# Attention and experts on one core: another order for the first three pairs of heads

## The chip, the cores and the metric

The kernel runs on one core of a Trainium2 chip. The metric is the device time in microseconds (us) of one execution, as the median of several runs. Beside those runs one execution was profiled: its trace tells for every engine when each instruction ran. The engines are TensorE (PE; its weight loads are shown apart as PEld), VectorE (DVE), ScalarE (ACT), GpSimd (POOL) and SyncE (SP), which issues most of the transfers.

## The reference

The program is an attention over 64 heads, and behind it a routed expert layer. The change touches the attention alone. Its arithmetic is this (8 batches of 8 heads, 1152 keys of 64 elements, queries pooled in twos to 576):

```python
def _attn_ref(q, k, v) -> np.ndarray:
    B, H, S, D = q.shape
    factor = 2
    scale = 1.0 / np.sqrt(D)
    q_pool = q.reshape(B, H, S // factor, factor, D).mean(axis=3)
    scores = scale * np.matmul(q_pool, k.transpose(0, 1, 3, 2))
    scores = scores - np.max(scores, axis=-1, keepdims=True)
    attn = np.exp(scores)
    attn = attn / (np.sum(attn, axis=-1, keepdims=True) + 1e-09)
    return np.matmul(attn, v).astype(np.float32)
```

The result goes, as x of 4608 rows, to the expert layer: a gate product, a greedy assignment of each row to one of 8 experts with room for 576 rows each, and two products with a relu between them for each expert.

## The kernel before

The 64 heads are worked on as 32 pairs, numbered 0 to 31. A pair has 18 score steps, nine blocks of 128 keys for each of its two heads; step g of the program is step g mod 18 of pair g // 18. A step (function `step`) has four parts. PE makes the scores of 128 keys against 576 queries, four products into one of the two score banks `sc` (L751). ACT takes their exponential into a buffer P (L754). POOL, or for a few steps DVE, writes what the rounding of P leaves over into a buffer PM (L758). PE then multiplies P and PM with the values into a bank `av` (L768, 15 products; "AV" below). There are ten P and ten PM buffers. POOL takes the PM parts of all 18 steps of pair 0.

Softmax here doesn't subtract the exact maximum while scores come. Before a pair's scores start, an upper bound for each query is found. PE multiplies the pair's rounded queries and keys (L668, L678, for pair 0 L659) into the banks `ma` and `mb`, DVE takes the maximum of each (L671, L680, L662), folds the maxima (L703, for pair 0 L699) and, after a transposition on PE (L723, L713), writes them as extra rows that the scores take in (L724 and a transfer; for pair 0 L717 and L720). So the bounds of pair n+1 are made while the steps of pair n run. Keys and queries are split into a rounded half (KH, QH) and a rest (KL, QL), and spread to where the scores want them by transfers that SP issues (L617). Values are split in the same way (V; L634 to L645). From pair 2 on the rests are made by DVE (KL: L610, QL: L591, V: L645); for pairs 0 and 1 by POOL (L578 to L606, L638). Once a pair POOL also issues a transfer that adds the second query of each two to the first (L486).

What stands at the start besides: memsets on POOL (L459 to L463, among them the row of KB buffers that the extra rows are multiplied with, L461), and on PE 23 products of constants (L891, "fillers"), which are made for no result. Every second pair the finished attention output is transposed on PE (L803), copied by ACT (L806) and multiplied with the gate weights (L815).

The order on every engine is made ahead of the run by `Cycle.plan`: each item has a tag and a number within its tag and pair, a table gives a time for it, and items are taken by that time as soon as what they need has been taken. Table `TAU` is for all pairs, with 25 times the pair's number added; `TAU0`, `TAU1` and `TAU2` hold the entries of pairs 0, 1 and 2. Engines and queues work in the order so written: an instruction that waits holds up all that stand behind it on its engine, and a transfer that waits holds up SP's later ones.

Of the kernel before, what the change touches and what calls it, by code (L numbers as in the profile page):

```python
# [152 lines left out]
class Cycle(Order):  # L153
# [11 lines left out]
    def plan(self):  # L165
# [44 lines left out]
       [2.7664, 4.9823, 6.5534, 8.0795, 9.6086, -181.5656, 16.9348, 19.0221, 21.216], "qkb": [5.2308, 7.0644, 8.3738,  # L210
       12.1143, 0.0557, 20.0132, 22.5039, 25.3261, 28.3165], "ql": [-38.1313], "rc": [9.2364, -9.47], "sc":
       [-36.4174], "scv": [-30.065], "spr": [-21.9235, -31.1405, -21.9627, -26.5265, -22.5479, -164.2155, -315.3032,
       -74.6622, -15.1485, -17.1123, -19.956, -16.4269], "store": [-95.7261], "sx": [16.3692, 22.2312, 0.8466,
       -61.2066, -78.1894], "tab": [-60.4], "tad": [-127.8336], "tap": [-44.6145, -41.1498, -47.4908, -31.2065],
       "vh": [-26.7285, -47.8828], "vl": [-23.1603, -21.3115], "vs": [-148.6017, -208.4574], "vsh": [-168.3274],
       "wsq": [12.8365], "x": [-94.3595, -7.6786]}
TAU0 = {"abk": [-60.377, -62.9993], "abs": [-96.8953, -53.0217], "aug": [-7.39949, -0.804], "augt": [-7.399491,
# [133 lines left out]
def attention(ctx, tc, top, kt, qt, v, wg, w1, x_dram, L, npair=NPAIR):  # L351
# [3 lines left out]
    od = Cycle()  # L355
# [1295 lines left out]
```

## Time and profile before

| what | value |
|---|---|
| median of 3 runs | 1245.68 us (1243.24 to 1245.83) |
| the profiled execution | 1244.15 us, its span in the trace 1242.4 us |
| busy share of the span | PE 96%, DVE 82%, ACT 78%, POOL 73% |
| first exponential of pair 0 | 26.62 us |
| 19th, 37th, 55th, 73rd exponential | 63.50, 90.70, 114.25, 136.58 us |
| attention, 576 exponentials | to about 780 us; the expert layer after that |

The 19th, 37th, 55th and 73rd exponentials mark where pairs 1, 2, 3 and 4 begin. Later on a pair takes 22.3 or 23.4 us in turn; the first three take 36.9, 27.2 and 23.6 us.

### The profile page before, as it was taken

What the parts mean: (1) busy time and instruction counts of PE and PEld (TensorE: products, weight loads), DVE (VectorE), ACT (ScalarE), POOL (GpSimd) and SP (SyncE); (2) the same over time, 40 slices, a digit from 0 to 9 for tenths busy, and PEclk for the clock granted to TensorE, in tenths of its full rate; (3) what the DMA queues carried; (4) which work ended last, traced back from release to release, by engine and by line L of the source; (5) the groups of instructions that cost most, each with busy time, mean ns of one, the idle gap of its engine ahead of it and who ended that gap; (6) DMA issues with size and microseconds to landing.
All of it is one profiled execution on the core that took longest, in us unless ns stands there. A gap on an engine that the chain in (4) does not pass through costs nothing.

```text
span 1242.4 us, 38895 instructions
## 1 busy us (share of the span) xinstructions
PE 1193.8 (96%) x15470; PEld 862.5 (69%) x15470; DVE 1020.9 (82%) x2743; ACT 973.7 (78%) x1719; POOL 901.8 (73%) x879
## 2 busy tenths in 40 slices
PE   7899999998999999999999999789999999999998
PEld 2567777777777787777777778565657466575663
DVE  5889999999999899999999995689888898893520
ACT  6879999998999899999999987055876686776751
POOL 5879898897888898888897898044775584665641
PEclk7999999999999999999999999899999999999999
DMA  6677676776676777776876741042453554547401
GB/s 185 161 177 193 168 186 178 181 188 162 164 183 184 169 179 183 177 179 176 187 185 164 182 98 39 20 174 82 131 192 108 165 183 137 170 135 228 122 31 39
DMA packets 131218, 190.83 MB, mean 154 GB/s; under 512 B 50268, under 2 KB 86108, under 8 KB 128732
## 3 DMA queue, kind: packets, MB, share of 16 engines
q1 hardware_dynamic: 117948, 126.75, 38.8%
q0 software_dynamic: 12944, 61.58, 17.7%
q8 instruction: 121, 1.98, 0.7%
q14 instruction: 61, 0.50, 0.1%
q10 hardware_dynamic: 144, 0.02, 0.0%
HBM read 116.41 MB, written 18.87 MB: 109 GB/s over the span
## 4 chain that ended last, share of the span: by engine, by line
PE 77%; DVE 11%; DMA 5%; ACT 3%; issue 2%; POOL 1%; SPq 0%; POOLq 0%; ACTq 0%; DVEq 0%
PE sc L751 21%; PE av L768 18%; PE ph L1536 11%; PE po L1566 10%; PE mb L668 5%; PE ma L668 5%; DMA W<-in_w_dram,widx 2%; DVE MX L671 2%; PE av L803 1%; ACT P L754 1%; PE av L815 1%; PE rt L1169 1%; DVE HX L1545 1%; DVE GE L1163 1%; PE po L1572 1%
## 5 line engine op out<-in xcount | busy, mean ns | idle before, releaser
L758 POOL TENSOR_TENSOR PM<-P 128x576 f16<-128x576 f32 x508 | 614.3, 1270 | 103.9 <-ACT P L754 53.3
L754 ACT ACTIVATE P<-sc,EX 128x576 f32<-128x576 f32 x576 | 412.8, 739 | 80.4 <-PE sc L751 65.3
L768 PEld LDWEIGHTS <-P 128*128 128x128 bf16 x5760 | 294.5, 98 | 30.6 <-issue 2.3
L768 PE MATMUL av<-V,P 128*128 128x65 f16 (+1 forms) x5760 | 302.7, 192 | 0.0
L768 PE MATMUL av<-V,PM 128*128 128x65 f16 x2880 | 294.1, 194 | 0.0
L768 PEld LDWEIGHTS <-PM 128*128 128x128 f16 x2880 | 264.2, 97 | 0.0
L751 PE MATMUL sc<-QB,KB 65*128 65x288 f16 (+1 forms) x1152 | 236.6, 286 | 0.8 <-DMA QB<-AU 0.8
L751 PE MATMUL sc<-QA,KA 128*128 128x288 f16 x1152 | 235.3, 285 | 1.6 <-ACT P L754 1.3
L671 DVE TENSOR_REDUCE MX<-mb 128x1 f32<-128x512 f32 x279 | 191.0, 685 | 29.2 <-PE mb L668 23.9
L671 DVE TENSOR_REDUCE MX<-ma 128x1 f32<-128x512 f32 x279 | 191.0, 685 | 11.0 <-PE ma L668 7.5
L751 PEld LDWEIGHTS <-KA 128*128 128x128 f16 x1152 | 106.4, 97 | 75.9 <-issue 23.6
L1566 PE MATMUL po<-W2H,HX 128*128 128x512 f16 x512 | 155.5, 379 | 0.0
L1536 PE MATMUL ph<-XH,W1H 128*128 128x320 f16 (+1 forms) x512 | 146.2, 286 | 1.1 <-ACT XH L1425 0.6
L1536 PE MATMUL ph<-XL,W1H 128*128 128x320 f16 (+1 forms) x512 | 146.2, 286 | 0.6 <-DVE XL L1430 0.6
L1536 PE MATMUL ph<-XH,W1L 128*128 128x320 f16 (+1 forms) x512 | 145.9, 286 | 0.0
L751 PEld LDWEIGHTS <-KB 65*128 65x128 f16 (+1 forms) x1152 | 112.8, 98 | 30.9 <-issue 1.0
L1566 PEld LDWEIGHTS <-HX 128*128 128x128 f16 x768 | 71.2, 98 | 78.5 <-issue 0.5
L1536 PEld LDWEIGHTS <-W1H 128*128 128x128 f16 x1024 | 97.9, 98 | 31.0 <-issue 6.4
L1588 POOL DMA_INDIRECT out_dram<-OT,idx x40 | 39.0, 975 | 109.8 <-ACT OT L1568 91.8
L668 PE MATMUL mb<-KH,BD 128*128 128x512 f16 x279 | 106.1, 380 | 6.3 <-DVE AU L724 4.0
L668 PE MATMUL ma<-KH,BD 128*128 128x512 f16 x279 | 106.3, 381 | 4.4 <-DVE MX L671 1.8
L1489 POOL TENSOR_TENSOR W2L<-W,W2H 128x512 f16<-128x512 f32 x64 | 73.1, 1157 | 38.6 <-ACT W L1487 34.1
(308 smaller groups left out, 2159.7 us busy)
## 6 DMA issues: line engine op xcount, KB each, us to landing
KD<-in_kt_dram SPq DMA_DIRECT2D x64, 288.0 KB
VD<-in_v_dram SPq DMA_DIRECT2D x32, 576.0 KB
WB<-in_w_dram SPq DMA_DIRECT2D x32, 512.0 KB
QA<-QH SPq DMA_DIRECT2D x128, 72.0 KB
KA<-KH SPq DMA_DIRECT2D x64, 144.0 KB
KA<-KL SPq DMA_DIRECT2D x64, 144.0 KB
KB<-KH SPq DMA_DIRECT2D x64, 144.0 KB
x_dram<-X SPq DMA_DIRECT2D x16, 576.0 KB
```

What stands on the lines that cost most here:

```text
L668: od.add(t, "PE", 214, lambda: nc.tensor.matmul(m, BD[i][:, j, :], KH[i][:, 512 * c:512 * c + 512], start=True, stop=True), r=bd + [("KH", ...
L671: od.add(t, "DVE", 597, lambda: nc.vector.tensor_reduce(MX[i][:, j, c:c + 1], m, axis=AX.X, op=OP.max), r=[mk], w=[("MX", i, j, c)], tag=" ...
L751: nc.tensor.matmul(c[:, t, :288], a[i][:rows, s, ks], b[i][:rows, s, 288 * t:288 * t + 288], start=first, stop=not first)
L754: od.add(g + 0.1, "ACT", 624, lambda: nc.scalar.activation(p.rearrange("p (t q) -> p t q", t=2), c[:, :, :288], AF.Exp, scale=EX[n % 3][:, ...
L758: od.add(g + 0.2, en, dur, lock=1, fn=lambda: eng.tensor_tensor(pm, p, hi, op=OP.subtract), r=[("P32", g % NP)], w=[("PM", g % NM)], tag="pm")
L768: nc.tensor.matmul(out, w[:, qs], v, start=kb == 0 and j == 0 and y == 0, stop=kb == NKB - 1 and y == 2, skip_group_check=True)
L803: nc.tensor.transpose(m[:, 128 * z:128 * z + 128], X[u][:, 3 * q + z], ident)
L815: nc.tensor.matmul(av[1][32 * q:32 * q + E, :384], wgs[:, c], XT[q].rearrange("p c t -> p (c t)"), start=True, stop=True)
L1489: od.add(tt, "POOL", 1230, lambda o=lo[p], a=raw[p], h=hi[p]: nc.gpsimd.tensor_tensor(o, a, h, op=OP.subtract), r=[key, hk, sk], w=[(nm + ...
L1536: nc.tensor.matmul(p, a[:, d, fs], b[:, d, qs], start=z == 0, stop=z == 11)
L1566: nc.tensor.matmul(o, a[:, z, q0:q0 + 128], b[:, z], start=z == 0 and y == 0, stop=z == 7 and y == 2)
L1588: st = nc.gpsimd.indirect_dma_start(out=out, out_offset=bass.IndirectOffsetOnAxis(ap=idx[i][:n, c:c + 1], axis=0), in_=OT[ob][:n], in_offs ...
```

## The change

The tables `TAU0`, `TAU1` and `TAU2` are written anew, and now hold entries for the score steps of pairs 1 and 2 as well, which took those of `TAU` before. In `TAU` three entries are other numbers: `kh` (the first half of the rounded keys), `kl`, and `gt` (the second of the three gate transpositions). For pair 0 the bound products of the first head go through five banks in a fixed turn (ma, av0, sc0, av1, sc1) where eight were used by a running number. Two starting values of pair 1's items change with it.

Of the tables two lines stand here for all:

```diff
-       [-94.8433], "gt": [23.9764, 39.0716, 42.6939], "kh": [-31.3132, -34.1197], "kl": [-42.4384, -155.424], "ld":
+       [45.877], "gml": [37.3972, 54.4199, 340.2916], "gp": [-94.8433], "gt": [23.9764, 39.35, 42.6939], "kh":
+       [-32.4, -34.1197], "kl": [-32.38, -155.424], "ld": [-70.8466, -187.4708], "ldq": [-65.2457], "ldv":
...
@@ -651,10 +676,10 @@
         i = n % 2
         if n == 0:
             h, j = j // 5, j % 5
-            banks = [(ma, "ma"), (mb, "mb")]
-            if not h:
-                banks += [(sc[a // 2][:, a % 2], ("sc", a // 2, a % 2)) for a in range(4)] + [(av[b], f"av{b}") for b in range(2)]
-            m, mk = banks[z % len(banks)]
+            if h:
+                m, mk = ((ma, "ma"), (mb, "mb"))[z % 2]
+            else:
+                m, mk = ((ma, "ma"), (av[0], "av0"), (sc[0][:, 0], ("sc", 0, 0)), (av[1], "av1"), (sc[1][:, 0], ("sc", 1, 0)))[(5 * c + j) % 5]
...
             if n == 1:
-                at.update(load=-61.5, vload=-57, split=-42.5, bound=-42, spread=-34, val=-36, mm=-20, fold1=1, aug=1.5)
+                at.update(load=-61.5, vload=-57, split=-31.6, bound=-31.15, spread=-23.5, val=-29, mm=-20, fold1=1, aug=1.5)
...
     for g in range(npair * NSTEP):
         od.cur = od.base = g // NSTEP
-        od.zero = int(g < NSTEP)
+        od.zero = (1, 2, 3, 0)[min(g // NSTEP, 3)]
         step(g)
```

The change neither adds nor removes an instruction; line numbers behind the tables are 25 higher after it. From pair 3 on two things stand in another place: every second pair one ACT pass (KH) and one set of gate transpositions on PE. Three places follow.

The first is POOL where pair 0 ends (PM_157 from P_147 is the PM part of step 17, V_104 the rest of pair 1's values, KB_96 the buffer of pair 1 that L461 fills). Before:

```order
L758 TENSOR_TENSOR PM_155<-P_145 128x576
L758 TENSOR_TENSOR PM_157<-P_147 128x576
L758 TENSOR_TENSOR PM_156<-P_146 128x576
L638 TENSOR_TENSOR V_104<-VD_123,V_104 128x9x64 x2
L758 TENSOR_TENSOR PM_158<-P_148 128x576
```

Now:

```order
L783 TENSOR_TENSOR PM_151<-P_141 128x576
L663 TENSOR_TENSOR V_104<-VD_123,V_104 128x9x64 x2
L783 TENSOR_TENSOR PM_153<-P_143 128x576
L783 TENSOR_TENSOR PM_154<-P_144 128x576
L511 DMA QS_125<-in_qt_dram 128x576
L783 TENSOR_TENSOR PM_155<-P_145 128x576
L783 TENSOR_TENSOR PM_156<-P_146 128x576
L783 TENSOR_TENSOR PM_157<-P_147 128x576
L486 MEMSET KB_96 9x2304
L783 TENSOR_TENSOR PM_159<-P_149 128x576
```

The rests of pair 1's values moved from behind pair 0's last PM part to five parts before its end, and the fill of KB_96 from the start of the program to behind that last part.

The second is PE where pair 1's scores begin (the AV products of step 17 stand right ahead; BD_101 and KH_85 are operands of pair 2's bounds, KA_94 and QA_98 of pair 1's scores). Before:

```order
L668 LDWEIGHTS BD_101
L668 MATMUL ma<-KH_85,BD_101 128x512
L668 LDWEIGHTS BD_101
L668 MATMUL mb<-KH_85,BD_101 128x512
L668 LDWEIGHTS BD_101
L668 MATMUL ma<-KH_85,BD_101 128x512
L668 LDWEIGHTS BD_101
L668 MATMUL mb<-KH_85,BD_101 128x512
L668 LDWEIGHTS BD_101
L668 MATMUL ma<-KH_85,BD_101 128x512
L751 LDWEIGHTS KA_94
L751 MATMUL sc_166<-QA_98,KA_94 128x288
```

Now:

```order
L793 MATMUL av_169<-V_103,PM_157 128x65
L776 LDWEIGHTS KA_94
L776 MATMUL sc_167<-QA_98,KA_94 128x288
L776 LDWEIGHTS KA_94
L776 MATMUL sc_167<-QA_98,KA_94 128x288
L776 LDWEIGHTS KB_96
L776 MATMUL sc_167<-QB_100,KB_96 128x288
L776 LDWEIGHTS KB_96
L776 MATMUL sc_167<-QB_100,KB_96 128x288
L776 LDWEIGHTS KA_94
L776 MATMUL sc_166<-QA_98,KA_94 128x288
```

Five bound products of pair 2 stood ahead of pair 1's first scores; now four score steps of pair 1 come first, and pair 2's bounds behind them.

The third is ACT in every second pair from pair 4 on (KH_85 is a half of the rounded keys of the pair after next, XT the copy of the gate transpositions). Before:

```order
L806 COPY XT_163<-av_169 128x384
L754 ACTIVATE P_140<-sc_166,EX_116 128x576
L754 ACTIVATE P_147<-sc_167,EX_116 128x576
L806 COPY XT_164<-av_169 128x384
L601 ACTIVATE KH_85<-KD_119,SC_115 128x576
L754 ACTIVATE P_142<-sc_166,EX_116 128x576
```

Now:

```order
L831 COPY XT_163<-av_169 128x384
L779 ACTIVATE P_140<-sc_166,EX_116 128x576
L779 ACTIVATE P_147<-sc_167,EX_116 128x576
L626 ACTIVATE KH_85<-KD_119,SC_115 128x576
L831 COPY XT_164<-av_169 128x384
L779 ACTIVATE P_142<-sc_166,EX_116 128x576
```

The second half of the keys is rounded one place earlier, ahead of the copy XT_164.

## Rows read from the trace of the kernel before

**Rows 1.** Windows: start:end, length; busy (count) PE, PEld, DVE, ACT, POOL; clock; DMA

```profile
10.00:26.62 16.62, 14.09 (x40) 4.15 (x39) 10.85 (x28) 10.61 (x18) 10.33 (x8) 0.50 0.67 176
26.62:63.50 36.88, 31.06 (x394) 19.62 (x394) 29.34 (x60) 29.34 (x51) 28.66 (x28) 0.96 0.60 144
63.50:90.70 27.20, 24.28 (x328) 17.67 (x327) 22.09 (x41) 21.45 (x38) 20.28 (x21) 0.92 0.70 176
90.70:114.25 23.55, 23.54 (x388) 18.37 (x385) 21.82 (x44) 21.34 (x39) 20.71 (x31) 1.00 0.80 196
114.25:136.58 22.33, 22.33 (x379) 17.95 (x376) 20.77 (x43) 20.95 (x39) 20.39 (x19) 1.00 0.65 167
273.78:300.73 26.95, 23.67 (x387) 18.32 (x385) 25.22 (x44) 21.42 (x39) 20.18 (x19) 1.00 0.67 167
```

**Rows 2.** Timeline, first scores: start, length, engine, line, tiles, [idle before <-releaser]

```profile
18.86 1.89 PE L891 MATMUL av<-wide,ones 128*128 128x512 bf16 x4
...
23.35 0.48 PE L713 MATMUL mb<-ident,CM 128*69 128x128 f32 x1
```

**Rows 3.** Timeline of DVE: the fold of pair 0's first head

```profile
19.79 0.17 DVE L699 TENSOR_REDUCE CM<-MX 128x4 f32<-128x12 f32 x1
```

**Rows 4.** Timeline of POOL: a fill of KB, and pair 0's work

```profile
15.79 2.01 POOL L461 MEMSET KB<- 9x2304 f16 x1
...
33.12 1.28 POOL L606 TENSOR_TENSOR KL<-KD,KH 128x576 f16<-128x576 f32 x1 [0.32 <-ACT KD L604]
...
36.70 4.46 POOL L758 TENSOR_TENSOR PM<-P 128x576 f16<-128x576 f32 x4
41.10 0.85 POOL L486 DMA_DIRECT2D QS<-in_qt_dram  x1
...
54.82 1.15 POOL L758 TENSOR_TENSOR PM<-P 128x576 f16<-128x576 f32 x1 [0.63 <-ACT P L754]
59.90 2.42 POOL L638 TENSOR_TENSOR V<-VD,V 128x576 f16<-128x576 f32 x2 [3.93 <-ACT VD L636]
```

**Rows 5.** Timeline of DVE: fold of pair 1; pair 2's first maximum; fold of pair 2

```profile
53.60 0.18 DVE L703 TENSOR_REDUCE CM<-MX 128x9 f32<-128x27 f32 x1
...
59.88 0.69 DVE L671 TENSOR_REDUCE MX<-ma 128x1 f32<-128x512 f32 x1 [0.21 <-PE ma L668]
...
82.77 0.17 DVE L703 TENSOR_REDUCE CM<-MX 128x9 f32<-128x27 f32 x1
```

**Rows 6.** Timeline of PE: pair 2's first bound product

```profile
59.47 0.38 PE L668 MATMUL ma<-KH,BD 128*128 128x512 f16 x1 [1.49 <-DMA BD<-QH]
```

**Rows 7.** Windows of L768 (PE and PEld alone): nine AV steps ahead of pair 1

```profile
54.60:59.50 4.90, 3.35 (x105) 3.25 (x105) 1.00 0.33 48
```

**Rows 8.** Windows: all engines while pair 2's bounds are made

```profile
59.88:82.77 22.89, 20.56 (x256) 13.94 (x255) 20.47 (x36) 19.91 (x35) 17.99 (x19) 0.93 0.79 200
```

**Rows 9.** Timelines of ACT, PE, DVE, POOL: pair 4 at the gate transpositions

```profile
150.18 0.48 ACT L806 COPY XT<-av 128x384 f32<-128x384 f32 x1
150.56 0.78 ACT L601 ACTIVATE KH<-KD,SC 128x576 f16<-128x576 f32 x1
...
151.37 0.82 DVE L610 SCALAR_TENSOR_TENSOR KL<-KD,SC,KH 128x576 f16<-128x576 f32 x1
...
151.37 0.87 POOL L486 DMA_DIRECT2D QS<-in_qt_dram  x1
...
152.53 0.82 PE L815 MATMUL av<-XT,wgs 128*8 128x384 f32 x6
```

**Rows 10.** Timelines of POOL and DVE: the same place in pair 10

```profile
288.57 0.89 POOL L486 DMA_DIRECT2D QS<-in_qt_dram  x1
289.20 3.65 POOL L758 TENSOR_TENSOR PM<-P 128x576 f16<-128x576 f32 x3
...
288.88 4.59 DVE L610 SCALAR_TENSOR_TENSOR KL<-KD,SC,KH 128x576 f16<-128x576 f32 x1 [0.25 <-issue]
```

**Rows 11.** The line L610: count, shortest, median and longest in ns

```profile
L610 DVE SCALAR_TENSOR_TENSOR KL<-KD,SC,KH x60: 802/814/4587, 56.9 to 730.0; 128x576 f16<-128x576 f32 x60
```

More of the change, by code (lines that the diff above doesn't have):

```diff
@@ L215 @@
-       "vh": [-26.7285, -47.8828], "vl": [-23.1603, -21.3115], "vs": [-148.6017, -208.4574], "vsh": [-168.3274],
-       "wsq": [12.8365], "x": [-94.3595, -7.6786]}
-TAU0 = {"abk": [-60.377, -62.9993], "abs": [-96.8953, -53.0217], "aug": [-7.39949, -0.804], "augt": [-7.399491,
[5 rows of a table removed]
-        -7.026297, 1.533201, 4.734301, 9.325501, 23.883701], "expb": [-7.399487, -7.399467, -7.399445, -7.399424,
-        1.198702, 3.416501, 5.503401, 22.1687, 22.168703], "fill": [-10.2794, -126.6764, -30.3842, -147.957,
-        -245.9624, -174.4366, -139.2362, -212.3909, -147.5215, -160.7165, -141.2792, -181.6421], "fold": [-7.399497,
[11 rows of a table removed]
-        1.5332, 4.7343, 9.3255, 23.8837], "qkb": [-7.399488, -7.399468, -7.399446, -7.399425, 1.198701, 3.4165,
-        5.5034, 13.319, 22.168702], "ql": [-29.9917], "qs": [-147.1978], "rc": [9.181703, 25.133714], "sc":
-        [-60.376997], "scv": [-37.467499], "spr": [-60.376977, -38.883998, -35.21, -60.37698, -31.0808, -29.991699,
[6 rows of a table removed]
@@ L246 @@
-TAU1 = {"abs": [-34.9327, -39.4214, -46.3877], "aug": [-1.025495], "augd": [-1.025494, -1.025493], "augt":
[6 rows of a table removed]
-        -16.355199, -23.751799, -15.081299, -21.213299, -10.492399, -18.345799, -13.433399, -1.025498], "mre":
-        [-27.9644, -1.0255, -8.404399], "qa": [-68.5572], "qh": [-32.399481], "ql": [-28.143899], "sc": [-32.399483],
-        "scv": [-24.0828], "spr": [-32.39945, -9.0591, -32.399452, -32.399477, -17.2565, -9.3805, -32.399451, -1.8944,
-        -32.399453, -32.399478, -32.399476, -5.7004], "vd": [1.4358, 1.435801], "vh": [-24.082798, -24.082799], "vl":
-        [1.435803, 1.435802], "vs": [-32.399489, -32.399485], "vsh": [-32.399484]}
@@ L258 @@
-TAU2 = {"abs": [-44.485199, -38.0633, -27.5185], "aug": [-0.158697], "augd": [-0.158696, -0.158695], "augt":
[10 rows of a table removed]
[2 rows of a table added]
+       [13.4958, -71.9751, -301.8994, -63.224, -198.6406, -15.9845, -78.5836, 33.7202, -197.7787], "bdd":
+       [-52.3637, -285.2947], "best": [30], "el": [-77.0706], "ex": [-50.7557], "expa": [-16.6599, -154.184,
+       -20.8529, 5.9927, 12.6026, 14.7889, -14.7359, -29.1238, -104.9479], "expb": [-32.523, -130.2187,
[11 rows of a table added]
+       4.9823, 6.5534, 8.0795, 9.6086, -181.5656, 16.9348, 19.0221, 21.216], "qkb": [5.2308, 7.0644, 8.3738,
@@ new lines @@
+       12.1143, 0.0557, 20.0132, 22.5039, 25.3261, 28.3165], "ql": [-38.1313], "rc": [9.2364, -9.47], "sc":
+       [-36.4174], "scv": [-30.065], "spr": [-21.9235, -31.1405, -21.9627, -26.5265, -22.5479, -164.2155,
+       -315.3032, -74.6622, -15.1485, -17.1123, -19.956, -16.4269], "store": [-95.7261], "sx": [16.3692,
+       22.2312, 0.8466, -61.2066, -78.1894], "tab": [-60.4], "tad": [-127.8336], "tap": [-44.6145, -41.1498,
+       -47.4908, -31.2065], "vh": [-26.7285, -47.8828], "vl": [-23.1603, -21.3115], "vs": [-148.6017,
@@ new lines @@
+       -208.4574], "vsh": [-168.3274], "wsq": [12.8365], "x": [-94.3595, -7.6786]}
+TAU0 = {"abk": [-158.8971, -154.1632], "abs": [-18.36343, -4.432959], "aug": [-83.38275, -166.4732], "augt":
[5 rows of a table added]
+        -31.28967, -16.54009, 11.37296, -165.2382, 7.395536, -8.984111, -4.211814], "expb": [-29.09149,
+        -22.94875, -1.956318, -58.58073, -17.31112, 8.70511, -44.15053, -10.60943, -83.61574], "fill":
[13 rows of a table added]
+        -0.7874408, -89.24226, -30.95353, -90.94815, 19.75168], "qkb": [-38.71843, -25.8134, -10.06655, 9.20107,
+        -67.31496, -58.03232, -88.79007, 19.41297, 27.0304], "ql": [-118.7245], "qs": [-143.2866], "rc":
+        [-32.42996, -52.99154], "sc": [-118.7466], "scv": [13.52603], "spr": [-12.95725, -60.11802, -17.91313,
+        -33.7785, -32.93921, -13.53914, 7.216188, -42.886, 4.220658, -38.88641, -146.5483, -24.13281], "vd":
+        [-49.85137, -34.44854], "vh": [8.519713, -90.95726], "vl": [-18.40057, -17.39675], "vs": [-142.1097,
+        -10.46893, -117.9683, -53.38023], "vsh": [-33.54066], "wsq": [12.26831], "wu": [-17.875, -17.555,
+        -17.235, -16.915, -16.595, -16.275, -15.955, -15.635, -15.315, -14.995], "wx": [-4.689, -4.369, -3.886,
+        -3.403, -3.083, -2.763, -2.28, -1.797, -1.314, -0.994, -0.674, -0.354, -0.034], "x": [26.86098,
+        -21.42417]}
@@ new lines @@
+TAU1 = {"abs": [-12.63603, -9.007276, -10.61048], "aug": [-9.325879], "augd": [-24.68238, -15.56411], "augt":
[5 rows of a table added]
+        "expa": [-31.62902, -34.53196, 7.506785, -5.098975, -3.698539, -9.956472, 18.47283, -146.9597,
+        -8.541267], "expb": [-92.73379, -23.81719, -29.00838, -7.55417, 15.52308, 17.65719, 20.07963, -36.40239,
+        -8.822007], "fold": [-67.48551], "kd": [-17.85042, -20.86023, -101.4387], "kh": [-21.38899, -13.56883],
+        "kl": [-24.3647, -69.39262], "ld": [-38.975, -38.325], "ldq": [-40.925], "ldv": [-39.625], "ldw":
[8 rows of a table added]
+        7.957536, -30.97699, 26.53293], "qkb": [-134.6881, -19.11279, 4.672508, 7.631733, -18.85315, -7.293164,
+        -146.6946, -45.59129, 22.34192], "ql": [-46.37856], "rc": [-86.19829, -10.06201], "sc": [-61.60109],
+        "scv": [-12.29273], "spr": [-7.110299, -82.23665, -9.971891, -10.88851, -4.162817, -38.01306, -24.27872,
+        -157.8473, -11.66528, -19.92012, 9.739897, -18.36458], "vd": [-13.48229, -158.5643], "vh": [-13.8261,
+        -115.4854], "vl": [-32.5142, -145.3052], "vs": [-102.0759, -147.1307], "vsh": [-42.73812], "wsq":
+        [11.82567], "x": [13.33649, -21.05682]}
@@ new lines @@
+TAU2 = {"abs": [-28.66554, -33.20308, -33.07647], "aug": [-155.8978], "augd": [-31.13019, -15.26595], "augt":
[5 rows of a table added]
+        [-36.73381, -17.79995, 11.0648, 12.05918, 4.224331, -49.88403, -79.15411, -73.20015, -78.03694], "expb":
+        [5.303638, -28.09439, -86.66189, 11.14589, 13.52404, 0.9933214, -108.1325, 17.65723, -12.04455], "fold":
+        [-76.7964], "kh": [-25.48746, -30.72508], "kl": [-85.91257, -137.1086], "ld": [-43.77507, -60.36052],
+        "ldq": [-155.8887], "ldv": [-44.13215], "ldw": [-36.80441], "me": [-14.41274, -10.50764, -4.941736],
[7 rows of a table added]
+        [3.525368, 5.485969, 7.082238, -29.81771, 16.89603, 17.62602, 19.72256, 21.49451, 25.15933], "qkb":
[4 rows of a table added]
+        -140.0679], "vsh": [-156.7671], "wsq": [25.35071], "x": [-88.3642, 9.707762]}
```

8 lines of the change are left out of this document (removed), and 106 rows, old and new, of tables (TAU, TAU0, TAU1, TAU2).

## The prediction

> **What bounds the kernel now.** I read first the windows cut at the first exponential of each pair [rows 1]. From pair 3 on PE is busy through the whole window (22.33 of 22.33 us), so nothing but PE's own work sets the time there, and a change of order can win little. The first three windows are another matter: 36.88, 27.20 and 23.55 us for pairs that later take 22.3 to 23.4. In pair 0 PE is idle for 36.88 - 31.06 = 5.8 us and in pair 1 for 2.9 us by this count; and the count flatters PE, since a product that runs at the lower clock counts as busy for longer. What stands above the later pairs is 36.88 + 27.20 + 23.55 - 3 x 22.85 (the mean of 22.33 and the 23.4 that the next pair takes) = 19 us, of which a part is work that only pair 0 has (the fifteen bound products of its second head). That is what could be won here.
>
> Next I looked in the timelines at what ended last before each pair's first scores. For pair 0 it is the transposition of the first head's maxima: the fold is there at 19.79 [rows 3], the transposition comes at 23.35 [rows 2], since on PE it stands behind products of the second head, each of which waits for DVE to empty its bank, and behind fillers (1.89 us for four [rows 2]). For pair 1 it is PE's own order: the fold is at 53.60 [rows 5], and nine AV steps behind it are done near 59, but then stand five bound products of pair 2, the first of which waits 1.49 us for a transfer [rows 6], and the others for DVE; the scores follow, and the exponential is at 63.50. For pair 2 it is DVE: its bounds begin at 59.88 and are folded at 82.77 [rows 5], 22.9 us, of which DVE is busy for 20.47 [rows 8]; the pair begins at 90.70, 7.9 us behind its fold.
>
> Last, the later pairs: one is out of line. Pair 10 takes 26.95 us where its neighbours take 22.33 [rows 1], 4.6 us more. Its cause is one DVE instruction: a KL pass of 4.59 us [rows 10], where the median of 60 is 0.81 [rows 11]. It stands beside three PM parts of POOL without a gap between them (3.65 us), behind POOL's transfer issue at 288.57.
>
> **The change part by part.** No instruction is added or removed, so every term is a wait.
>
> *First scores of pair 0.* In the new order no product of the second head stands ahead of the transposition, only the first head's fifteen and fillers. Five of the ten early fillers now stand behind the first sums and ahead of the first bound product, which begins some 0.4 us later; five banks in place of eight cost DVE little, as it takes one bank after the other anyway. If the fold comes as before or 1.5 us later (19.8 to 21.3), and a group of five fillers (1.89 / 4 x 5 = 2.4 us) lies partly beside it, the transposition is at 20.2 to 23.7 in place of 23.35. I take 21.9, 1.5 us earlier, so pair 0 begins at 25.1. Ends: -3 and +0.3.
>
> [...]
>
> *Pair 1.* Two chains end here now. On POOL: 18 PM parts at 4.46 / 4 = 1.115 us, three rests of keys and queries at 1.28, one transfer issue of 0.85, and now also the rests of pair 1's values, 2.42 [rows 4]: 20.1 + 3.8 + 0.9 + 2.4 = 27.2 us. It starts with the first exponential's end, 25.1 + 0.7 = 25.8, so ends at 53.0 without a gap. Before, POOL's last PM part of the pair ended at 54.82 + 1.15 = 55.97 [rows 4], 28.6 us behind its first exponential's end, for about 26 us of such work; with the same 2.7 us of gaps it is 55.7. Behind it stands the fill of KB_96, 2.01 us [rows 4], without which pair 1's scores can't start: 55.0 to 57.7. On PE: the fold of pair 1, then nine AV steps. 105 recorded products of them took 3.35 us [rows 7], so 135 take 4.3. DVE works off the second head of pair 0 first and then pair 1's bounds, the same number as before; with pair 0 earlier I put the fold at 51 (49 to 53.6), plus 0.9 for transposition and rows, plus 4.3: 56.2 (54.2 to 58.8). What covered the fill before was its place at the start; that cover is gone, and it now ends level with PE's chain. I take 56.5 for the scores and 57.2 for the exponential: 6.3 us earlier than 63.50. Ends: -8.5 and -4. On SP the load of the next values now waits for those value rests, with six transfers of pair 1's keys and queries behind it; the rests end five PM parts and an issue before the chain does, near 47, so these land in time.
>
> *Pair 2.* Its bounds begin behind four score steps of pair 1, the third and fourth of which each wait for an exponential: about 58.8, only 1.1 us earlier than 59.88. But DVE has less in that stretch (one KL pass, one value rest and one maximum of pair 3, some 2 us, for one QL pass of 0.8), and the 2.4 us of idle time [rows 8] come mostly from two bound products in a row on one bank, of which the new order has fewer. I put the length at 20.5 (19 to 22.9) and the fold at 79.3; with 6.1 us from fold to scores and exponential (7.9 before, since the last score steps and fewer AV steps stand between) pair 2 begins at 85.3: -5.4. Ends: -2 and -8.
>
> *Pair 3.* Pair 2 is bound by PE before (23.54 of 23.55) and stays so. Some three of its 18 AV steps are done before it begins, 1.4 us; the rest of its work is the same: 22.4 us in place of 23.55. Pair 3 begins at 107.7, **6.6 us** earlier, and all behind it with it. Ends: -3 and -10.
>
> *Later pairs.* In pair 4 the KL pass and POOL's issue begin at the same time to 10 ns, 151.37, the first as soon as the KH pass is done (150.56 + 0.78 = 151.34) [rows 9]. In pair 10 the issue came first, and the pass waited for all that POOL had behind it [rows 10]. Now KH stands ahead of a copy of 0.48 us, so KL no longer waits for it, and comes at the place that DVE's own order gives it. In 59 of 60 cases the pass got through [rows 11], so this is worth what pair 10 lost, 26.95 - 22.33 = **4.6 us**, if it doesn't come back elsewhere; ends -4.6 and 0. [...] The moved gate transpositions swap with one bound product of a saturated PE: nothing.
>
> *Sum.* Against the profiled execution's 1244.15 us: -6.6 - 4.6 gives **1233.0**. That execution lies 1.5 below the median of the runs shown, whose spread of 2.6 us may well be such lost ties; I don't add the difference.
>
> **The rivals.** *The tie is no part of it:* other executions don't lose it, or it is lost in another pair as often. For it: 1 of 60; against it: the issue and the pass at one time in the rows. 1244.15 - 6.6 = 1237.6.
>
> *POOL takes the place of what was removed:* its chain in pair 0, now 29.2 us with values and fill, gets gaps (exponentials that wait for ACT, which also has pair 1's keys then), or pair 2's bounds, begun later against pair 1's scores, take the 22.9 us of before. Then the first three pairs win 2 to 3 us. For it: POOL is busy for 28.66 us of pair 0, almost as long as DVE and ACT [rows 1]; against it: most of DVE's 2.4 us of idle is PE's order, which changes. With the tie 1237.5, without it 1242.
>
> [...]
>
> *Slower:* on ACT the copy XT_164 now stands behind the KH pass, so 0.7 us later in every second pair. If the gate products (L815) wait for it, PE loses up to 0.7 us in 14 pairs, 9.8: 1244.15 - 6.6 + 9.8 = 1247.4. It decides from the point where the copy ends behind L815's start; before, it ends at 150.66 and L815 starts at 152.53 [rows 9], 1.9 us of slack against 0.7. That speaks strongly against it.
>
> **How the numbers follow.** Forecast 0.48, first three pairs alone 0.27, POOL's or DVE's chain 0.14 (half of it with the tie), clock 0.05, slower 0.06. Own ranges: 1229.5 to 1236.5 for the forecast; 1234 to 1241 for the second. The range is 1229 to 1241.5, which leaves out the slower case and part of the third. No change is what lies within 0.2%, 2.5 us. Faster: 0.48 + 0.27 + 0.05 and 0.09 of the third case, 0.89; within: 0.04 of the third and 0.02 of the slower case, 0.06; slower: the rest of both, 0.05.
>
> **What would show it.** In the profile of the changed kernel: the first exponential near 25.1; the 19th near 57.2, with POOL's fill of KB_96 just ahead of pair 1's first scores; the 37th near 85 and the 55th near 108; the later pairs at 22.3 and 23.4 in turn, none near 27, and no KL pass over 2 us. Wrong would be a 19th exponential behind 60, a gap of PE at L815, or later pairs that are longer than before.

## The result, and the profile after

The changed kernel takes 1232.34 us (median of four runs, 1230.94 to 1237.53), the kernel before 1244.62 beside it (four runs, 1243.24 to 1245.83): a ratio of 0.990, with an interval of 0.987 to 0.993. The forecast of 1233.0 is 0.7 us off. Its terms fared less well than their sum.

The profiled execution of the changed kernel is the slowest of the four, 1237.53, with a span of 1235.8. Its windows, cut at the first exponentials of pairs 0, 1, 2, 3 and 4, and around pair 10, with the columns of [rows 1]:

```profile
10.00:25.13 15.13, 13.43 (x41) 3.58 (x40) 10.55 (x27) 11.85 (x20) 10.58 (x13) 1.00 1.02 260
25.13:56.35 31.22, 28.08 (x393) 18.57 (x393) 24.61 (x55) 28.37 (x49) 28.90 (x25) 1.00 0.52 136
56.35:84.23 27.88, 24.72 (x348) 17.59 (x346) 25.33 (x49) 21.36 (x38) 20.01 (x21) 1.00 0.61 143
84.23:109.90 25.67, 24.42 (x377) 18.17 (x376) 24.35 (x45) 21.45 (x38) 21.65 (x32) 1.00 0.79 205
109.90:132.74 22.84, 22.31 (x377) 17.82 (x374) 20.46 (x42) 20.86 (x39) 19.84 (x18) 1.00 0.66 164
269.83:293.20 23.37, 23.37 (x388) 18.33 (x385) 21.53 (x44) 21.23 (x39) 20.16 (x19) 1.00 0.76 192
```

Against [rows 1] the first exponential comes 1.5 us earlier, pair 0 is 5.7 shorter, pair 1 is 0.7 and pair 2 is 2.1 longer; pair 3 begins 4.35 earlier. Pair 10 is 3.6 shorter. Where pair 31 begins (750.96, before 759.72) 8.8 us are won. The span is only 6.6 shorter: PE waits longer for the first gathered rows of the expert layer (XG, rows that a transfer collects for an expert). PE's timeline of the changed kernel there:

```profile
814.89 1.12 PE L1410 MATMUL po<-ident,XG 128*128 128x128 f32 x4 [3.72 <-DMA XG<-x_dram,idx]
```

Before, the same wait was 1.89, and in a second profile of the changed kernel 1.98; behind the last exponential every engine has the same instructions in the same order in both kernels.

The first part, in PE's timeline (L916 are the fillers, L738 the transposition, L776 the scores) and in VectorE's (the folds of pairs 0, 1 and 2):

```profile
18.40 2.31 PE L916 MATMUL av<-wide,ones 128*128 128x512 bf16 x5
...
21.31 1.25 PE L916 MATMUL av<-wide,ones 128*128 128x512 bf16 x5
22.84 0.30 PE L738 MATMUL mb<-ident,CM 128*69 128x128 f32 x1 [0.27 <-DVE CM L725]
...
24.43 0.42 PE L776 MATMUL sc<-QA,KA 128*128 128x288 f16 x2
```

```profile
22.47 0.17 DVE L724 TENSOR_REDUCE CM<-MX 128x4 f32<-128x12 f32 x1
...
50.47 0.18 DVE L728 TENSOR_REDUCE CM<-MX 128x9 f32<-128x27 f32 x1
...
77.96 0.18 DVE L728 TENSOR_REDUCE CM<-MX 128x9 f32<-128x27 f32 x1
```

Five fillers take 2.31 us at 18.40 and 1.25 at 21.31, and the trace's records of the granted clock begin at 21.2, with 1.00: PE came to this higher clock near 21, where before it stayed at 0.50 to 26.6 [rows 1]. The 1.00 of the first window above doesn't show this: the trace holds no record of the clock before 21.2, and a stretch without one counts as 1.00. The transposition now waits for the fold and not for PE's order. Pair 1's scores (POOL's fill, then PE):

```profile
52.89 2.01 POOL L486 MEMSET KB<- 9x2304 f16 x1
```

```profile
55.57 0.19 PE L793 MATMUL av<-V,PM 128*128 128x65 f16 x1
55.60 0.28 PE L776 MATMUL sc<-QA,KA 128*128 128x288 f16 x1
```

The fill ends at 54.90, the ninth AV step is issued just before 55.60: PE's chain is the later one, by 0.7. Pair 2 is where time went back. VectorE and POOL there:

```profile
92.50 1.46 DVE L783 TENSOR_TENSOR PM<-P 128x576 f16<-128x576 f32 x1
...
97.34 1.74 DVE L635 SCALAR_TENSOR_TENSOR KL<-KD,SC,KH 128x576 f16<-128x576 f32 x1
...
99.92 0.18 DVE L728 TENSOR_REDUCE CM<-MX 128x9 f32<-128x27 f32 x1
100.02 1.63 DVE L635 SCALAR_TENSOR_TENSOR KL<-KD,SC,KH 128x576 f16<-128x576 f32 x1
```

```profile
97.33 1.15 POOL L783 TENSOR_TENSOR PM<-P 128x576 f16<-128x576 f32 x1 [0.68 <-ACT P L779]
...
99.89 2.76 POOL L783 TENSOR_TENSOR PM<-P 128x576 f16<-128x576 f32 x2 [0.20 <-ACT P L779]
```

Each KL pass begins just behind the begin of a PM part of POOL (by 0.02 and 0.12 us) and takes twice the usual 0.81. Ahead of these passes PE had waited for maximum banks that VectorE had not emptied; such products otherwise begin some 0.22 us before the next one:

```profile
90.16 0.38 PE L693 MATMUL mb<-KH,BD 128*128 128x512 f16 x1
90.72 0.38 PE L693 MATMUL ma<-KH,BD 128*128 128x512 f16 x1 [0.18 <-DVE MX L696]
91.32 0.38 PE L693 MATMUL mb<-KH,BD 128*128 128x512 f16 x1 [0.22 <-DVE MX L696]
```

These two waits and a third at 89.46 cost PE 1.0 us from begin to begin, the late fold 0.8. The line's summary over all pairs (compare [rows 11]), and PE at the transposition that waits for the late fold:

```profile
L635 DVE SCALAR_TENSOR_TENSOR KL<-KD,SC,KH x60: 803/808/1741, 53.9 to 721.3; 128x576 f16<-128x576 f32 x60
```

```profile
100.15 0.28 PE L748 MATMUL mb<-ident,CM 128*9 128x128 f32 x1 [0.66 <-DVE CM L728]
```

No pass takes 4.6 us any more.

### The profile page after: what moved, and what is told of

Its sections match the earlier page's. It is cut to its first block, busy times and chain, and to the rows that moved or that the text cites. A ratio compares the mean times of both kernels' runs of the same rounds, so it can differ in the third digit from the quotient of the medians.

```text
span 1235.8 us, 38902 instructions
## 1 busy us (share of the span) xinstructions
PE 1190.0 (96%) x15470; PEld 860.7 (70%) x15470; DVE 1018.7 (82%) x2743; ACT 972.0 (79%) x1719; POOL 901.6 (73%) x879
## 3 DMA queue, kind: packets, MB, share of 16 engines
q8 instruction: 121, 1.98, 0.7%
## 4 chain that ended last, share of the span: by engine, by line
PE 77%; DVE 13%; DMA 4%; issue 2%; ACT 2%; POOL 0%; SPq 0%; POOLq 0%; ACTq 0%; DVEq 0%
PE sc L776 20%; PE av L793 18%; PE ph L1561 11%; PE po L1591 11%; PE mb L693 4%; PE ma L693 4%; DVE MX L696 3%; PE av L828 1%; DMA BD<-QH 1%; PE av L840 1%; ACT P L779 1%; DMA W<-in_w_dram,widx 1%; PE po L1597 1%; PE rt L1194 1%; DVE HX L1570 1%
## 5 line engine op out<-in xcount | busy, mean ns | idle before, releaser
L779 ACT ACTIVATE P<-sc,EX 128x576 f32<-128x576 f32 x576 | 412.6, 739 | 76.0 <-PE sc L776 58.8
L776 PE MATMUL sc<-QA,KA 128*128 128x288 f16 x1152 | 234.5, 285 | 1.4 <-ACT P L779 1.3
L776 PE MATMUL sc<-QB,KB 65*128 65x288 f16 (+1 forms) x1152 | 235.7, 285 | 0.0
L776 PEld LDWEIGHTS <-KA 128*128 128x128 f16 x1152 | 106.2, 97 | 73.1 <-issue 22.7
L776 PEld LDWEIGHTS <-KB 65*128 65x128 f16 (+1 forms) x1152 | 112.5, 98 | 29.4
```

The lines of the kernel that those rows point to most:

```text
L776: nc.tensor.matmul(c[:, t, :288], a[i][:rows, s, ks], b[i][:rows, s, 288 * t:288 * t + 288], start=first, stop=not first)
L779: od.add(g + 0.1, "ACT", 624, lambda: nc.scalar.activation(p.rearrange("p (t q) -> p t q", t=2), c[:, :, :288], AF.Exp, scale=EX[n % 3][:, ...
```

## Experiments

The runs were made on several chips, on which the kernel before took 1243 to 1268; so ratios to it, measured beside each run, are given with their intervals. Profiles of single executions are compared by the lengths of pairs.

**The changed kernel again** (no edit).

> The changed kernel as it is, profiled again. Theory (the first three pairs and the lost ties give the gain; what the first profiled execution lost in pair 2 and ahead of the expert layer was chance): 1232.3, the third pair shorter than the 25.67 us of the first profile (23 to 24), no two-input pass of DVE over 1.3 us between 84 and 110 us, and the wait for the first gathered rows near 1.9 us in place of 3.7. Rival (the new order itself makes DVE lose against POOL in pair 2): the long passes are there again, at 1.4 to 1.8 us each, and the third pair takes 25.7 again; then a profiled execution is also about 1236.

Ratio 0.990 [0.987, 0.993]. Pair 2 takes 25.67 us again, with the same passes (1.45, 1.74, 1.63), so the rival holds: this loss belongs to the new order. The wait for gathered rows was 1.98 here; over the 14 profiles of this document it is 0.7 to 3.9, and nothing shows that it belongs to the order. Pair 0 took 34.10 in place of 31.22. The windows of this run there:

```profile
28.00:31.00 3.00, 2.36 (x16) 1.21 (x15) 2.14 (x9) 2.89 (x7) 3.00 (x4) 1.00 0.00 0
31.00:34.00 3.00, 2.96 (x11) 1.05 (x10) 1.60 (x3) 2.44 (x4) 3.00 (x4) 0.50 0.34 55
34.00:37.00 3.00, 3.00 (x43) 2.30 (x42) 1.20 (x4) 2.49 (x4) 3.00 (x4) 0.50 0.41 126
37.00:40.00 3.00, 2.17 (x27) 1.54 (x24) 1.82 (x4) 0.32 (x1) 2.14 (x2) 0.86 0.52 145
```

The granted clock fell to 0.50 from 31 to some 38 us, in the same order that kept it in the first profile; this costs 2.9 us. Pair 3 then begins at 112.29, only 2.0 us earlier than in [rows 1].

**The three entries of TAU, alone and taken out.**

```diff
-"gt": [23.9764, 39.0716, ...], "kh": [-31.3132, ...], "kl": [-42.4384, ...]
+"gt": [23.9764, 39.35, ...], "kh": [-32.4, ...], "kl": [-32.38, ...]
```

> The kernel before with nothing but the three new entries of TAU (kh, kl, gt). Theory of the prediction (the rounded keys ahead of XT_164 take the KL pass out of the tie with POOL's transfer issue): no KL pass over 2 us in the profile, and a time 0 to 4.6 us below the kernel before, 1242 as the middle. Rival (the tie is no part of it): the time of the kernel before, 1244.6, within 0.5. Rival (the later XT_164 delays the gate products): 1246 or more.

Ratio 1.002 [0.999, 1.004]: no gain. Pair 10 takes 28.49. VectorE and POOL there:

```profile
286.17 0.18 DVE L703 TENSOR_REDUCE CM<-MX 128x9 f32<-128x27 f32 x1
286.60 4.70 DVE L610 SCALAR_TENSOR_TENSOR KL<-KD,SC,KH 128x576 f16<-128x576 f32 x1 [0.25 <-issue]
```

```profile
286.40 0.89 POOL L486 DMA_DIRECT2D QS<-in_qt_dram  x1
287.03 3.65 POOL L758 TENSOR_TENSOR PM<-P 128x576 f16<-128x576 f32 x3
```

KH was done 0.77 us ahead, and the fold began 0.23 before POOL's issue; elsewhere a pass begins 0.1 behind its fold's begin. It lost all the same, behind the same stop of 0.25 as in [rows 10]. My mechanism is refuted.

This profile shows one thing more. But for the three entries it has the old order in its first pairs, and here the old order came to the higher clock at 20.8 and kept it. Its windows for pairs 0, 1 and 2:

```profile
25.36:61.47 36.11, 29.71 (x393) 19.35 (x394) 28.70 (x59) 29.34 (x51) 28.68 (x28) 1.00 0.63 154
61.47:88.80 27.33, 23.15 (x328) 16.68 (x327) 23.54 (x42) 21.40 (x39) 19.72 (x20) 1.00 0.63 158
88.80:112.16 23.36, 23.36 (x388) 18.33 (x385) 22.00 (x44) 21.24 (x40) 22.86 (x32) 1.00 0.89 217
```

The first exponential comes at 25.36 in place of 26.62, and pair 3 begins at 112.16 in place of 114.25. Against this profile the changed kernel's first one gains 4.9 us in pair 0, loses 0.55 and 2.3 in pairs 1 and 2, and begins pair 3 only 2.3 earlier.

> The changed kernel with the three old entries of TAU. Theory of the prediction: the first three pairs keep their gain, 6 to 9 us, and KL passes tie with POOL's transfer issue again in every second pair, so 1232 to 1237, with one KL pass of some 4.6 us where an execution loses a tie. Rival (the tie is no part of it): the time of the changed kernel, 1232.3, within 1. Rival (the tables of the first pairs give little and the three entries most): above 1240.

Ratio 0.994 [0.992, 0.996]; the interval meets that of the changed kernel. In its profile KL passes begin within 6 ns of POOL's issue in nearly every second pair, and none loses (longest behind pair 3: 0.82). So the tie isn't what the entries change. The medians of this kernel and the changed one on the same chip are 3.3 us apart, and part of that is in the traces. In pair 1 of this kernel two KL passes meet PM parts of POOL, where they take 0.81 in the changed one:

```profile
72.09 1.70 DVE L635 SCALAR_TENSOR_TENSOR KL<-KD,SC,KH 128x576 f16<-128x576 f32 x1
...
75.70 1.57 DVE L635 SCALAR_TENSOR_TENSOR KL<-KD,SC,KH 128x576 f16<-128x576 f32 x1
```

Pair 1 takes 29.66 in place of 27.88. What else the entries do stays open.

**A place in VectorE's instruction stream.** Counted from 0 in the trace, waits for semaphores among them, the pass that lost is VectorE's record 575 in both profiles of the old order. In the changed kernel the same pass is record 579. With the three old entries of TAU it is 579 too, so the four records come from the new tables of the first pairs. So I moved the records and left the order as it was:

```diff
     nc.vector.memset(wide, 1.0)
+    pad = const.tile([128, 1], F32, name="pad")
+    for _ in range(4):      # 41 in the second
+        nc.vector.memset(pad, 0.0)
```

> The kernel before with four instructions more on VectorE at the program's start (memsets of one column of a tile that nothing reads, while VectorE waits for the first loads); all else stands in the same order. Theory (the stop of 0.249 us ahead of the KL pass of pair 10, seen in two profiled executions of the old order, belongs to a place in VectorE's instruction stream, and lets POOL's transfer issue go first): the place now falls four instructions earlier, no KL pass takes over 2 us, pair 10 takes 23.4 us, and the time is 3.6 below the kernel before, 0.997 of it. Rival (the pass loses by the engines' times alone): the KL pass of pair 10 takes 4.6 us again, pair 10 takes 27 to 28.5, time as before.

Ratio 0.9954 [0.9936, 0.9972]; no KL pass over 0.83 in the later pairs, pair 10 takes 23.38. Four idle instructions bring the old kernel 0.46%, while its first three pairs gain nothing (pair 3 begins at 115.44).

> The changed kernel with 41 such memsets on VectorE at the program's start, so that the second KL pass of pair 9, the 534th record of VectorE there, comes to the place 575, where the pass that lost stood in the old order. Theory (a place in the instruction stream): a stop of about 0.25 us ahead of that pass, which then takes some 4.6 us, and pair 9 takes 26 to 27 us in place of 22.4: 3.6 to 4.6 us slower than the changed kernel, 1.003 to 1.004 of it. Rival (the engines' times alone): no long KL pass, the time of the changed kernel.

Ratio 1.001 [0.999, 1.003], so some 14 us more than the changed kernel. VectorE in pair 9:

```profile
266.62 0.18 DVE L731 TENSOR_REDUCE CM<-MX 128x9 f32<-128x27 f32 x1
267.05 4.58 DVE L638 SCALAR_TENSOR_TENSOR KL<-KD,SC,KH 128x576 f16<-128x576 f32 x1 [0.25 <-ACT SC L571]
```

The loss came to the pair where it was sent: pair 9 takes 27.95 in place of 22.41. (The profile names ACT here, which had long been done.) The memsets themselves cost 3 us of the start, which I had taken to be covered. With the 5.5 of pair 9 that is 8.6 of the 14; the rest isn't accounted for.

The later runs met the same place unasked, 512 records on, at record 1087; VectorE in pair 21 of the run with TAU0 alone and of the first with moved KL passes (both below):

```profile
580.71 4.56 DVE L611 SCALAR_TENSOR_TENSOR KL<-KD,SC,KH 128x576 f16<-128x576 f32 x1 [0.25 <-ACT SC L544]
```

```profile
540.31 4.55 DVE L637 SCALAR_TENSOR_TENSOR KL<-KD,SC,KH 128x576 f16<-128x576 f32 x1 [0.25 <-ACT SC L570]
```

The stop costs more where the clock falls behind it. In the first profile of the old order the granted clock stayed at 1.00, and pair 10 grew by 3.6 us. In the run with the entries alone and in that with 41 memsets it fell to 0.50 for 3.4 us (from 293.9, from 272.4), and the pair grew by 5.1 and 5.5; in these last two runs it fell for 6.8 us, and pair 21 grew by 6.6. The window of the last:

```profile
544.50:551.00 6.50, 4.96 (x34) 3.33 (x34) 4.04 (x10) 2.19 (x4) 1.15 (x1) 0.50 0.42 102
```

In the 14 profiles there are 390 KL passes that stand right behind a fold. Five of them are at a record 63 above a multiple of 128, and these five lose; no other takes over 2 us. The page of the changed kernel counts transfers of instructions in two queues (pieces, MB, share), 16.4 and 8.2 KB a piece, without telling for which engine:

```profile
q8 instruction: 121, 1.98, 0.7%
q14 instruction: 61, 0.50, 0.1%
```

The page counts 38902 instructions, and 2.48 MB in both queues, so some 64 bytes each; by that a piece of q14 holds 128 of them (an estimate), and a period of 128 fits it. That the stop is VectorE waiting for such a piece is a guess that no row shows. Where a longer instruction stands ahead of the place, no stop is seen (0.68 us ahead of record 831 in the kernel before, 0.28 ahead of 1087 in the changed one); but there is none either at record 1727 of the kernel before, in the expert layer, which is also 63 above a multiple of 128 and stands behind instructions of 0.17 and 0.08 us.

**The tables one by one.** First TAU0 alone, with TAU1 and TAU2 of before (their lines are left out of the diff) and the steps of pairs 1 and 2 by TAU. The starting values of pair 1's items, of which the change has four new ones (split, bound, spread, val) and not two, stay new in both runs.

```diff
-        od.zero = (1, 2, 3, 0)[min(g // NSTEP, 3)]
+        od.zero = int(g < NSTEP)
```

> The changed kernel with TAU1 and TAU2 of the kernel before, and the steps of pairs 1 and 2 by TAU as there: of the tables of the first pairs only TAU0, with the five banks, is new. Theory (nearly all of the gain of the first three pairs lies in pair 0, whose order TAU0 sets: 36.9 before, 31.2 now, while pairs 1 and 2 together got longer, 50.8 to 53.6): pair 0 takes 31 to 33, pairs 1 and 2 take 27.2 and 23.6, and the 55th exponential comes at 107 to 109, 1 to 3 us earlier than in the changed kernel. Rival (the three tables hang together, and pair 1's items by the old entries fall at the wrong place in the new pair 0): pair 0 or pair 1 takes 3 to 10 us longer than now, slower than the changed kernel.

Ratio 1.030 [1.027, 1.032]. First exponential at 37.32, pair 0 59.78 long. What PE waits for (total, times, longest; 5 to 130 us), and the window of pair 0:

```profile
PE sc L752 <- ACT P L755: 8.0, 5, 6.5
PE mb L516 <- ACT VJ L504: 5.9, 1, 5.9
```

```profile
37.32:97.10 59.78, 43.76 (x390) 24.59 (x390) 28.08 (x59) 26.63 (x46) 30.99 (x27) 0.64 0.37 93
```

The granted clock is 0.64 over pair 0, so a good part of its length is the lower clock, which the profile of the changed kernel doesn't have there.

Then TAU0 of before with all else new.

> The changed kernel with TAU0 of the kernel before; TAU1, TAU2, TAU's three entries and the five banks stay new. Theory from the run with TAU0 alone, which lost 38 us (the three tables hang together): pair 0 or pair 1 is 5 to 40 us longer than before, and the kernel slower than before. Rival (TAU1 and TAU2 carry a part of the gain by themselves): pair 0 at 36.9 as before, and the 55th exponential not later than 114.

Ratio 1.027 [1.024, 1.030]: first exponential at 30.00, pair 0 59.69, at a granted clock of 0.73. The tables are one order: half of it is over 30 us worse than either whole.

**Eight banks** as before, the rest as changed.

```diff
-                m, mk = (... five banks ...)[(5 * c + j) % 5]
+                m, mk = (... eight banks ...)[z % 8]
```

> The changed kernel with the eight banks of before for the first head's bound products of pair 0. Theory of the prediction (five in place of eight cost VectorE little, as it takes one bank after the other): first exponential within 0.5 of the 24.4 to 25.1 of the profiles of the changed order, pair 0 as long as there, same time. Rival (the fixed turn is what lets the planner alternate: with the old rule seven of the second head's products stand in a row on bank ma, each waiting for VectorE): pair 0 is 1.5 to 4 us longer, and the kernel slower by as much.

Ratio 1.019 [1.016, 1.022]: first exponential at 36.73, pair 0 51.87. Seven products stand in a row on ma; PE's timeline, two of them, and the window of pair 0:

```profile
25.23 0.32 PE L684 MATMUL ma<-KH,QH 64*128 64x384 f16 x1 [0.65 <-DVE MX L687]
26.20 0.38 PE L684 MATMUL ma<-KH,QH 64*128 64x384 f16 x1 [0.65 <-DVE MX L687]
```

```profile
36.73:88.60 51.87, 40.46 (x387) 23.72 (x387) 22.26 (x48) 28.94 (x50) 29.28 (x25) 0.61 0.28 65
```

While PE waits like this, the granted clock falls to 0.50 at 26.3, and it stays there to 77.5. If 6.8 us at that level cost 2.9, as in the second profile of the changed kernel, the 40.8 us of it in pair 0 cost some 17 (an estimate) of the 20.7 by which the pair grew: by this estimate the row on one bank begins the loss, and the clock is most of its size.

**The fill of KB_96** ahead of pair 0's first PM part.

```diff
-        27.86655, 5.699136, -84.03057], "fold": ...
+        14.5, 5.699136, -84.03057], "fold": ...
```

> The changed kernel with the fill of KB_96 ahead of pair 0's first PM part, where POOL is idle for 3.26 us; by the planner's rules pair 1's first four score steps then stand ahead of pair 0's last AV steps on PE, not behind them. Theory (pair 1's start is set by PE's chain, and nine AV steps of 4.1 us stand ahead of its scores): the 19th exponential comes 2 to 4 us earlier (52.5 to 54.5 in place of 56.35), but DVE's bounds of pair 2 wait for the rounded keys on ACT behind it, so pairs 2 and 3 begin at most 1.5 us earlier: 1231 to 1232.5. Rival (the fill's 2.01 us on POOL are on the path): -2.0, 1230.3. Rival (the scores now wait on PE for the transfer of pair 1's bound rows, and the AV steps behind them): +2, 1234.3.

Ratio 1.002 [1.000, 1.005], some 15 us more than the changed kernel on the same chip. The last rival holds, at many times its price. PE, and ACT behind it:

```profile
53.00 0.64 PE L776 MATMUL sc<-QA,KA 128*128 128x288 f16 x2 [4.04 <-DMA QA<-QH]
```

```profile
55.18 0.74 ACT L779 ACTIVATE P<-sc,EX 128x576 f32<-128x576 f32 x1 [5.82 <-PE mb L545]
```

Pair 1's scores now stand ahead of nine AV steps and wait 4 us for a transfer; the AV steps, the sums that ACT needs and by them the buffers of the exponentials all wait behind. Pair 1 grows from 27.9 to 39.1; the granted clock is 0.50 from 52.5 to 66.2, and a part of the growth is that. What the late fill gives is not POOL's time: it holds the planner back from taking the scores too early.

**Pair 2's passes.** First, POOL makes the PM part of step 4:

```diff
+        pd = [12] if n == 2 else pd
```

> The changed kernel with the PM part of step 4 of pair 2 on POOL; VectorE has one PM part in that pair in place of two. Theory (pair 2 is set by VectorE, whose two-input passes are held up by POOL's PM parts): VectorE is free 1.46 us earlier there, pair 2 takes 24.2 in place of 25.67, and the time is 1.5 below the changed kernel. Rival (POOL becomes the late one, since it has 1.15 more to do, or the KL passes lose the same time elsewhere): 25.7 again, no difference. Rival (pair 2 is set by PE's own work, as the prediction had it): no difference either, with VectorE idle for 1.5 us more.

Ratio 0.991 [0.989, 0.993]; pair 2 takes 25.80. VectorE there:

```profile
97.44 0.69 DVE L705 TENSOR_REDUCE MX<-mb 128x4 f32<-128x512 f32 x1 [0.97 <-PE mb L703]
...
98.65 1.40 DVE L616 SCALAR_TENSOR_TENSOR QL<-QS,SC,QH 128x576 f16<-128x576 f32 x1
99.97 1.70 DVE L635 SCALAR_TENSOR_TENSOR KL<-KD,SC,KH 128x576 f16<-128x576 f32 x1
```

VectorE's busy time in the pair fell from 24.35 to 23.25: the PM part is gone, and a QL pass now meets one of POOL's. Its idle time grew by 1.2, in part behind PE, and PE waits 1.2 for the fold in place of 0.7. So the rivals hold against the theory, but the run doesn't tell them apart. Next, the two KL passes of pair 4's keys later, in `plan`:

```diff
+            if tag == "kl" and base == 4:
+                return PERIOD * base - 29     # 23 in the second try
```

> The changed kernel with the two KL passes of pair 4's keys, which VectorE makes during pair 2, put behind the fold of pair 3's maxima and its rows (AU); all other engines' orders stay. Theory (pair 2 takes 25.7 in place of 22.4 because these passes, at 1.74 and 1.63 us against POOL's PM parts, hold up the fold, and PE waits 0.8 for it at the transposition): the fold comes 1.5 to 1.7 earlier after the pair's begin (14.1 in place of 15.7), the wait at the transposition is gone, pair 2 takes 24.6 to 25.0, time 0.8 to 1 below the changed kernel. Rival (the waits of PE for emptied banks at the pair's begin, 1.0 us, and PE's own work decide): 25.4 or more, no difference that a time can tell.

Ratio 1.000 [0.998, 1.003]. 6.6 us of it are the pass at record 1087 (pair 21: 29.11), since two waits for semaphores fewer stand ahead. Pair 2 takes 29.80. The fold comes 14.9 after its begin as expected and PE doesn't wait for it; but PE waits for the copy LS behind the passes, which again took 1.43 and 1.70 (behind that wait the granted clock falls to 0.50 for 3.4 us):

```profile
PE av L795 <- DVE LS L846: 2.8, 1, 2.8
```

> As the kernel with pair 4's KL passes moved, but with the passes further back (behind the copy LS of the gate product and the normalizing of X, in front of which the first attempt held up PE for 2.8 us), and with three memsets of one column on VectorE at the program's start, which put VectorE's records behind pair 4 back to the places that they have in the changed kernel. Theory: no KL pass lies at a place 575 or 1087, so pair 21 takes 22.6 again in place of 29.1 (-6.5) and no pass takes over 2 us behind pair 4; pair 2's fold comes 14.9 us after the pair's begin in place of 15.7 and PE doesn't wait for it or for LS, so pair 2 takes 24.8 in place of 25.7: 0.990 of the kernel before, or 0.8 us below the changed kernel. Rival for the place (the loss in pair 21 came from the engines' times): pair 21 takes 29 again, 0.995 or more. Rival for pair 2 (PE's own work and the waits for emptied banks): 25.5 or more.

Ratio 0.994 [0.991, 0.996]. The place holds: pair 21 takes 22.32, no KL pass over 1.70. Pair 2 takes 27.68, and pair 3 24.57: PE now waits 2.9 us for a maximum behind the passes, and the granted clock falls to 0.50 for 3.4 us, from 109.8. Three ways to spare VectorE at one point brought the wait at another. No version beat the changed kernel.

## Why the prediction was right, and where it was not

- *First scores of pair 0*: 25.1 forecast, 25.13 measured, 23.1 to 25.1 in seven profiles of this start. Two errors cancel: the fold comes at 22.47, later than the 19.8 to 21.3 that I allowed, but from the transposition on it takes 2.3 us in place of 3.3, at the higher clock. So the number is luck. The earlier clock, to which the chances give 0.05, came true as an event (near 21 us), without a gain beyond the forecast, and what raised it isn't shown: the old start, with the same fillers in the same order, came to the higher clock at 26.7, 25.5 and 20.8 in its three profiles, with the first exponential at 26.62, 25.86 and 25.36.
- *Pair 1*: 57.2 forecast, 56.35 measured. The fold at 50.47 (51), nine AV steps in 4.1 us (4.3). POOL's chain ended 2.8 us earlier than I had it, its gaps gone. Where the clock fell in pair 0 (a mean of 0.90), in two other profiles of this order, the pair took 34.10 and not 31.22; the forecast had no term for that.
- *Five banks cost little*: true, but I missed what they do. With eight, the planner lays seven products on one bank, and the clock falls to 0.50 while PE waits for it.
- *Pair 2's begin*: 85.3 forecast, 84.23 measured; bounds from 58.68 (58.8), fold at 77.96 (79.3).
- *Pair 3's begin*: 107.7 forecast, 109.90 measured. The step "Pair 2 is bound by PE before and stays so" failed. It took 25.67, not 22.4: three two-input passes of VectorE met POOL's PM parts, VectorE was busy for 24.35 us, and PE waited for it. These waits of PE are 1.8 us, 1.0 for emptied banks ahead of the KL passes and 0.8 for the fold behind one of them, so the passes are only a part of it; no run that spared VectorE made the pair shorter, and which of the two matters more stays open. The step "Some three of its 18 AV steps are done before it begins, 1.4 us" failed too: 260 AV products are recorded in the pair, 272 before, so less than one step (and 23.55 - 1.4 is 22.15, not 22.4). I had read POOL's and VectorE's hold on each other from pair 10 and didn't ask for it where the new order sets the two engines against each other anew. So this term is -4.35 between the two first profiles, not -6.6, and it depends on the clock: pair 3 begins at 109.90, 112.29 and 110.85 in three profiles of the new tables (the last with the old entries of TAU), and at 114.25, 115.44 and 112.16 in three of the old ones.
- *Later pairs*: the loss in pair 10 is gone, as forecast, but the step "Now KH stands ahead of a copy" is wrong: with KH moved alone the pass lost again. It lost by a stop at its place in VectorE's stream, and the change moved it off that place by four records that the first pairs' tables add, not by KH: the term came true by luck. The size was wrong too: pair 10 should have been set against other pairs of its parity, 23.38, so 3.6 and not 4.6; by whole runs, with four memsets, 4.8. The rival "the tie is no part of it" named the wrong alternative.
- *XT_164 later*: no wait at the gate products, as argued: PE's idle time ahead of all 84 of them is 3.3 us in both kernels, and none of it is ended by XT.
- *The sum*: -4.35 - 3.6 and about -0.8 in other pairs (pair 16 alone 1.0) give the 8.8 us up to pair 31. The medians differ by 12.3, and the ratio on another chip is the same. The rest stays open. The profiles see little of it: that of the changed kernel is of the slowest of its four executions, and no slower execution of the old order was profiled. A clock that the new order keeps more often would fit, but isn't shown. The mean granted clock of the timed runs is 0.974 to 0.995 in the old order and 0.988 to 0.997 in the changed one; between the two first profiles it is 0.985 and 0.993, and nearly all of that (16.62 us at 0.50, 0.007 of the span) is the start, which the changed kernel's trace leaves uncounted to 21 us. So of the forecast's two terms one was too large and the other right for a wrong reason, and the total was right by luck.

## What to carry to other kernels

When one of many equal instructions is slow, count its place in the engine's stream and look for its twin in a second profile before calling it chance: the same record in both is a cause that four idle instructions can test. Where VectorE and GpSimd both run two-input passes, read who begins first: 5 ns ahead of POOL's issue a KL pass lost nothing (0.82 us), 20 ns behind a PM part it lost 0.93 us. Read the granted clock beside every pair that grew, since a wait of PE and a fall of the clock behind it are two losses (with pair 4's KL passes moved, a wait of 2.8 us, then 3.4 us at 0.50). In an order that a table makes, an item that costs little can be there to hold others back, and a table can't be judged by halves.

## What the runs showed of the hardware that was not expected

A KL pass that began before POOL's issue took 0.81 us; one that began 20 ns behind a PM part's begin took 1.74; one that a stop of 0.25 put behind the issue took 4.55 to 4.70, until POOL had a gap behind three parts. VectorE's stop of 0.248 to 0.251 us appeared at records 575 and 1087, on at least three chips and in five kernels, each time behind instructions of 0.02 and 0.18 us; at the same records behind longer ones it did not (0.76 us at 575 and 0.28 at 1087 in the changed kernel).

The passes at 1.74 lost 0.93 us each, beside one PM part of 1.15; the five long ones lost 3.7 to 3.9, beside POOL's issue and three parts in a row.

The old start came to the higher clock at 20.8 us in one execution and at 26.7 in another. Pair 10's stop cost 5.1 us where the granted clock fell behind it (to 0.50 for 3.4 us), and 3.6 where it stayed at 1.00.
